# A new layout of the attention phase in front of two MoE layers, with three more weight pieces converted in it and their low parts passed through DRAM

## The chip, the core and the metric

The kernel runs on one core of one Trainium2 chip. The metric is the device time of one execution in microseconds (us), the median of several runs. Lower is better.

## What is computed

Attention over four batches, eight heads, 576 tokens and 64 columns a head, in two parts that are added: attention over queries, keys and values averaged in groups of four tokens (144 of them), repeated four times, and attention within three tokens to either side. Two dense layers follow on the 2304 x 512 result.

```python
out_d = sm_attn(q_d, k_d, v_d)                 # q_d, k_d, v_d: means over 4 tokens
out_up = np.repeat(out_d, factor, axis=2)
mask = np.abs(pos[:, None] - pos[None, :]) < factor
scores = np.where(mask, scale * np.matmul(q, k.transpose(0, 1, 3, 2)), -1000000000.0)
out_local = np.matmul(softmax(scores), v)
x = (out_up + out_local).transpose(0, 2, 1, 3).reshape(2304, 512)
h = x @ w_in;  r = np.maximum(h, 0.0);  x = (r * r) @ w_out          # layer 1, d_ff = 2048
h = x @ w_in2; y = (h * np.cos(h)) @ w_out2                          # layer 2
```

The weights are float64. The kernel turns each into a sum of two 32-bit numbers, a high and a low part.

## The kernel before

Layer 1 is cut into five blocks of tokens (8, 7, 7, 7 and 7 windows of 64 tokens) and 16 weight pieces of 128 hidden columns. A **slot** is one piece in one block: stage A (`stage_a`, 12 matmuls) makes the hidden tile `ps_h`, ScalarE makes `gt` and `gh` of it (`gelem1`, lines 543 and 544, `high`, line 532), VectorE makes `gl` (`low`, line 538), and stage B (`stage_b1`, 12 matmuls) adds to four accumulators. The time from the program's start to the first matmul of slot 0 is called the **first phase** here, and the 16 slots of the first block are **block 0**.

A weight piece is **converted** by `conv1` and `split`: its 1 MB raw tile is loaded by SP (line 413), ScalarE takes the absolute value of the top words into a tile `bits` (line 427), VectorE makes four passes over it (lines 429, 430, 434, 437), ScalarE rounds it to the high part `w1hi` (line 441), and GpSimd subtracts to get the low part in two halves, `loa` and `lob` (line 448), which stay in SBUF for block 0 and are also stored to DRAM (`lo_d`, line 473) for the later blocks. There are two raw tiles and two `bits` tiles.

Attention consists of tasks, written as Python generators that are advanced in turn: `pool` (the sums over four tokens), `down` (attention over these sums, one for each pair of heads; its results are the tiles `xd`, written at line 290) and `window` (the local attention of 64 tokens, four head pairs at once; its last steps add `xd` at line 388 and write the block's inputs `xh` and `xl` at lines 400 and 401). Windows 0 to 7 make block 0. While they are worked on (`early`), large temporary tiles are put into the places of weight pieces that are not yet converted (`spare`, `SPREAD`). `warm` puts matmuls without a use into the first phase: 48 at the start and 8 in each round of the tasks. In the first phase of the kernel before, piece 0 is converted early, piece 1 once six windows are ready and piece 2 once eight are.

Every engine runs its instructions in the order of the program, and that order was made by a list scheduler; DMAs are all issued by SP, in order, and an issue that waits holds back all behind it.

Of the kernel before, what the change touches and what calls it, by code (L numbers as in the profile page):

```python
# [42 lines left out]
AHEAD = 3  # L43
WARM0 = 48
WARM = 8
NA2 = 6
# [21 lines left out]
def kernel(  # L68
# [54 lines left out]
    def need(name, n=1):  # L123
        while early[0] and name in SPREAD:
            if spare:
                held.setdefault(name, []).append(spare.pop(0))
                return
            yield
        while used[name] + n > caps[name]:
            yield  # L130
        used[name] += n

    def done(name, n=1):
        if early[0] and name in SPREAD:
            spare.append(taken[name].pop(0))
        else:
            used[name] -= n

    spare = list(range(AHEAD, NF))
    held, taken = {}, {}  # L140

    def task_tile(name, rows, cols):
        if not early[0]:
            return cm.tile([rows, cols], F32, tag=name, name=name, bufs=caps[name])
        f = held[name].pop(0)
        taken.setdefault(name, []).append(f)
        return wp.tile([P, 2 * DM], F32R, tag=f"hi{f}", name=name).bitcast(F32)[:rows, :cols]
# [32 lines left out]
    def pool(b):  # L180
        yield from need("qp")
        yield from need("vp")
        kp = cm.tile([P, HPAIR, SD], F32, tag="kp", name="kp", bufs=caps["qp"])
        vp = cm.tile([KTOK, 2, DM], F32, tag="vp", name="vp", bufs=caps["vp"])
        parts = [(i, hp) for hp in range(HPAIR) for i in range(2)]
        parts += [((0, 1), hp) for hp in range(HPAIR)] if early[0] else [((kt,), hp) for hp in range(HPAIR) for kt in range(2)]
        loaded = []
        for i, hp in parts:
            yield from need("pl")
            if isinstance(i, int):  # L190
                t = task_tile("pl", P, S)
# [8 lines left out]
            if not early[0] and len(loaded) == 2:  # L200
                yield
                while loaded:
                    pool_sum(*loaded.pop(0), kp, vp)
                    done("pl")
        for piece in loaded:
            pool_sum(*piece, kp, vp)
            done("pl")
        pooled[b] = (qp, kp, vp)

    def pool_sum(*piece):  # L210
# [3 lines left out]
    def pool_piece(i, hp, t, kp, vp):  # L214
# [9 lines left out]
        else:  # L224
# [3 lines left out]
            )  # L228

    def down(b, hp):  # L230
        while b not in pooled:
# [15 lines left out]
        nc.vector.tensor_reduce(out=mx[:, 0], in_=sv, op=ALU.max, axis=AX.X)  # L247
        nc.vector.tensor_tensor(
            out=pr, in0=sv, in1=mx[:, 0].unsqueeze(2).broadcast_to([QROWS, 3, SD]), op=ALU.subtract
        )  # L250
        done_a(s)
        nc.scalar.activation(out=pr, in_=pr, func=AF.Exp, scale=SCALE / FACTOR ** 2)
        yield
        nc.vector.tensor_reduce(out=mx[:, 1], in_=pr, op=ALU.add, axis=AX.X)
        nc.vector.tensor_scalar(
# [51 lines left out]
    def window(w):  # L307
# [19 lines left out]
        for hp in range(HPAIR):  # L327
# [6 lines left out]
        prv = pr[:, :, :n]  # L334
        nc.vector.tensor_reduce(out=mx[:, 0], in_=sv, op=ALU.max, axis=AX.X)
        nc.vector.tensor_tensor(
            out=prv, in0=sv, in1=mx[:, 0].unsqueeze(2).broadcast_to([P, HPAIR, n]), op=ALU.subtract
        )
        done_a(s)
        nc.scalar.activation(out=prv, in_=prv, func=AF.Exp, scale=SCALE)  # L340
        yield
        nc.vector.tensor_reduce(out=mx[:, 1], in_=prv, op=ALU.add, axis=AX.X)
        nc.vector.tensor_scalar_add(out=mx[:, 1], in0=mx[:, 1], scalar1=1e-9)
# [21 lines left out]
        m = w - W0[j]  # L365
        while not early[0] and any((b, hp) not in downs for hp in range(HPAIR)):
            yield
# [86 lines left out]
    def conv1(f, after=0):  # L454
# [12 lines left out]

        for said in split(raw, hi1[f], ring):
            if said:
                done("raw")  # L470
            yield
        for k, lo in enumerate(los):
            nc.sync.dma_start(out=lo_d[f][:, k * DM:(k + 1) * DM], in_=lo.bitcast(F32))
# [197 lines left out]

    for f in range(AHEAD, NF):
        start_at(f - AHEAD - 1, conv1, f)
# [52 lines left out]
    for i in range(n1):  # L726
# [16 lines left out]
        jn, fn = divmod(i + AHEAD, NF)  # L743
        if jn > 0:
            for k in range(2):
# [112 lines left out]
```

## Time and profile before

| quantity | value |
|---|---|
| time, median of 3 runs (lowest to highest) | 1032.32 us (1029.2 to 1035.13) |
| time of the profiled execution | 1029.67 us |
| its span, first to last instruction | 1027.9 us |
| mean granted TensorE clock | 0.976 |
| TensorE matmul busy | 979.8 us, 95% of the span |
| VectorE busy | 615.3 us, 60% |
| ScalarE busy | 455.1 us, 44% |
| GpSimd busy | 140.4 us, 14% |
| first matmul of slot 0 | 90.40 us |

The shares are averages over stages that differ: TensorE is busy nearly always, but part of that is the matmuls without a use, and in the first phase it runs at a lower granted clock at times. VectorE's 60% is a mean of a first phase in which it often waits, a block 0 in which it hardly ever does, and long stretches later in which it has little to do.

### The profile page before, as it was taken

Reading aid. Unit: us, or ns where it says so; the run is one execution under the profiler, and the core shown is the slowest. Engines: PE = TensorE matmul, PEld = TensorE weight load, DVE = VectorE, ACT = ScalarE, POOL = GpSimd, SP = SyncE. Lnnn points to the kernel's source line nnn. Section 1 sums busy time; section 2 is a strip of 40 time slices with the busy share of each in tenths; the row PEclk is TensorE's granted clock in tenths of the full one; section 3 lists DMA queues with packets and bytes.
Section 4 is the critical chain, followed back from the end, with each engine's and each line's share of the span. In section 5 each row is a group of like instructions: output and inputs, shape, how many; then the busy total and the mean of one; then the engine's idle time right before and its main releaser. Section 6 shows DMA issues by size and latency. Waiting matters only on the chain.

```text
span 1027.9 us, 13081 instructions
## 1 busy us (share of the span) xinstructions
PE 979.8 (95%) x4868; PEld 825.8 (80%) x4868; DVE 615.3 (60%) x1062; ACT 455.1 (44%) x789; POOL 140.4 (14%) x112
## 2 busy tenths in 40 slices
PE   7879898889999999999999997999999999999998
PEld 4657677778999899999988895888888888888887
DVE  6628989967456844454227515756556555655565
ACT  2325555544555554444445434434334433433343
POOL 0301655511111221112003200000000000000000
PEclk9869999999999999999999999999999999999999
DMA  9903777775568856676556558001000100000010
GB/s 288 288 0 127 234 248 258 254 257 201 179 217 291 266 183 208 216 243 197 183 188 221 192 167 302 1 1 61 21 1 11 52 1 1 20 21 1 1 42 21
DMA packets 58096, 145.50 MB, mean 142 GB/s; under 512 B 6904, under 2 KB 12152, under 8 KB 53808
## 3 DMA queue, kind: packets, MB, share of 16 engines
q1 hardware_dynamic: 58032, 144.67, 42.2%
q8 instruction: 38, 0.62, 0.3%
q14 instruction: 26, 0.21, 0.1%
HBM read 116.33 MB, written 28.31 MB: 141 GB/s over the span
## 4 chain that ended last, share of the span: by engine, by line
PE 65%; DMA 7%; DVE 5%; ACT 2%; issue 1%; POOL 0%; SPq 0%; DVEq 0%; ACTq 0%
PE ps_h L520 30%; PE acc L578 19%; PE acc L572 11%; DMA pl<-in_pool_v_dram 2%; DMA pl<-in_pool_qk_dram 2%; DMA y_d<-y 2%; PE ps_a L372 1%; PE ps_a L328 1%; DVE bits L437 1%; DVE bits L434 1%; PE ps_a L281 1%; DVE gl L538 1%; DMA raw<-in_w_dram 1%; PE ps_a L355 1%; DVE vp L225 1%
## 5 line engine op out<-in xcount | busy, mean ns | idle before, releaser
L538 DVE TENSOR_TENSOR gl<-gt,gh 128x448 fp32r<-128x448 f32 (+1 forms) x80 | 58.4, 730 | 124.0 <-ACT gh L532 123.7
L520 PE MATMUL ps_h<-xh,w1hi 128*128 128x448 f32 (+1 forms) x320 | 124.1, 388 | 7.9 <-ACT gt L543 6.6
L572 PE MATMUL acc<-gl,w1hi 128*128 128x448 f32 (+1 forms) x320 | 121.4, 379 | 1.1 <-DVE gl L538 1.1
L520 PE MATMUL ps_h<-xh,w2hi 128*128 128x512 f32 (+1 forms) x320 | 118.2, 376 | 3.6 <-DVE r L564 3.6
L520 PE MATMUL ps_h<-xl,w1hi 128*128 128x448 f32 (+1 forms) x320 | 119.8, 374 | 0.0
L520 PE MATMUL ps_h<-xl,w2hi 128*128 128x512 f32 (+1 forms) x320 | 118.2, 376 | 0.0
L578 PE MATMUL acc<-w2hi,gh 128*128 128x512 f32 x288 | 113.9, 396 | 3.1 <-ACT y L587 2.5
L578 PE MATMUL acc<-w2lo,gh 128*128 128x512 f32 x288 | 113.4, 394 | 0.0
L560 ACT ACTIVATE r<-r,half_pi 128x512 f32<-128x512 f32 (+1 forms) x80 | 54.6, 683 | 132.0 <-DVE r L556 132.0
L578 PE MATMUL acc<-w2hi,gl 128*128 128x512 f32 x288 | 112.1, 395 | 0.0
L572 PE MATMUL acc<-gh,w1hi 128*128 128x448 f32 (+1 forms) x320 | 103.5, 381 | 2.3 <-ACT gh L532 2.0
L554 DVE TENSOR_SCALAR u<-u 128x512 f32<-128x512 f32 (+1 forms) x80 | 32.0, 399 | 121.0 <-ACT u L549 120.4
L572 PE MATMUL acc<-gh,lo 128*128 128x448 f32 x256 | 93.2, 364 | 0.0
L520 PE MATMUL ps_h<-xh,w2lo 128*128 128x512 f32 (+1 forms) x320 | 80.5, 372 | 0.0
L543 ACT ACTIVATE gt<-ps_h 128x448 f32<-128x448 f32 (+1 forms) x80 | 44.1, 552 | 76.3 <-PE ps_h L520 75.4
L520 PEld LDWEIGHTS ps_h<-xh,w1hi 128*128 128x128 f32 x320 | 61.2, 191 | 16.9 <-ACT gt L543 8.9
L520 PEld LDWEIGHTS ps_h<-xh,w2hi 128*128 128x128 f32 x320 | 60.6, 189 | 16.4 <-DVE r L564 4.1
L549 ACT ACTIVATE u<-ps_h,quarter 128x512 f32<-128x512 f32 (+1 forms) x80 | 51.5, 644 | 44.0 <-PE ps_h L520 41.6
L520 PEld LDWEIGHTS ps_h<-xl,w2hi 128*128 128x128 f32 x320 | 60.6, 190 | 12.3
L532 ACT ACTIVATE gh<-r 128x512 fp32r<-128x512 f32 (+1 forms) x80 | 47.1, 589 | 50.8 <-DVE r L564 46.0
L572 PEld LDWEIGHTS acc<-gh,w1hi 128*128 128x128 f32 x320 | 60.4, 190 | 10.0 <-ACT gh L532 2.6
L572 PEld LDWEIGHTS acc<-gl,w1hi 128*128 128x128 f32 x320 | 60.9, 190 | 8.8 <-DVE gl L538 2.6
(107 smaller groups left out, 1818.9 us busy)
## 6 DMA issues: line engine op xcount, KB each, us to landing
raw<-in_w_dram SPq DMA_DIRECT2D x32, 1024.0 KB
lo<-lo_d SPq DMA_DIRECT2D x128, 256.0 KB
qkw<-in_win_qk_dram SPq DMA_DIRECT2D x36, 396.0 KB
pl<-in_pool_qk_dram SPq DMA_DIRECT2D x32, 288.0 KB
w_d<-shi SPq DMA_DIRECT2D x10, 512.0 KB
w_d<-bits SPq DMA_DIRECT2D x10, 512.0 KB
w2lo<-w_d SPq DMA_DIRECT2D x10, 512.0 KB
w2hi<-w_d SPq DMA_DIRECT2D x10, 512.0 KB
```

Of the source, the lines that this page charges most:

```text
L225: nc.vector.tensor_reduce(out=vp[:, i[0]:i[-1] + 1, hp * P:(hp + 1) * P], in_=t.rearrange("p (k j r) -> p k j r", k=len(i), r=FACTOR), op= ...
L281: last["pe"] = nc.tensor.matmul(av[:, :2 * SD], vp[:, kt, hp * P:(hp + 1) * P], pt[:, kt], start=kt == 0, stop=kt == 1).ins
L328: last["pe"] = nc.tensor.matmul(sv[:, hp], qw[:, hp], kw[:, hp, :n], start=False, stop=hp == HPAIR - 1).ins
L520: nc.tensor.matmul(h[:, :n], a[:, c * P:(c + 1) * P], x[:, c, :n], start=i == 0, stop=i == len(order) - 1)
L532: nc.scalar.activation(out=gh, in_=gt, func=AF.Copy)
L538: last["gl"] = nc.vector.tensor_tensor(out=gl, in0=gt, in1=gh.bitcast(F32), op=ALU.subtract).ins
L543: last["relu"] = nc.scalar.activation(out=gt, in_=h, func=AF.Relu).ins
L549: nc.scalar.activation(out=u, in_=h, func=AF.Identity, bias=quarter, scale=float(1.0 / (2 * math.pi)))
L554: nc.vector.tensor_scalar(out=u, in0=u, scalar1=MAGIC, scalar2=MAGIC, op0=ALU.add, op1=ALU.subtract)
L560: nc.scalar.activation(out=r, in_=r, func=AF.Sin, bias=half_pi, scale=1.0)
L572: nc.tensor.matmul(acc[d][:, :n], a, x, start=f == 0 and i == 0, stop=f == NF - 1 and i == 2)
L578: nc.tensor.matmul(acc[t], x[:, ts], a[:, DM:2 * DM], start=f == 0 and i == 0, stop=f == NF - 1 and i == 2)
```

## The change

Only the first phase is written anew; the program from block 1 on is the same code.

- **Early softmax.** A new function `exps` is used by `down` and `window`. In the first phase VectorE only takes the maximum and scales it by a negative constant (a tiny operation); ScalarE then reads the scores from PSUM and takes the exponential with that value as bias, one instruction for each of three (`down`) or four (`window`) groups, with the sum as a second output. VectorE's subtraction over the whole tile and its sum over the whole tile go. Windows 8 and 9, which the scheduler also starts in the first phase, keep the old form.
- **Warm matmuls.** 48 become 32 at the start, 8 become 4 in each round.
- **Spare tiles.** The first two or three tiles of each kind of temporary (not `pl`) now come from their own pool; ten places of weight pieces are lent where 13 were, since pieces 3, 4 and 5 are to be converted.
- **Conversions.** Piece 0's is no longer put ahead; pieces 1 and 2 may start their passes once three and five windows are ready, and pieces 3, 4 and 5 (`PRE`) once six are, still in the first phase's task list. The low parts of these three are made in one GpSimd instruction in the `bits` tile, stored to DRAM, and read back by `load_lo` in slots 0, 1 and 2 for slots 3, 4 and 5.
- **Waits.** A window now waits for all `down` tasks of its batch ahead of its last product in the first phase too.
- `pe_pool` is there but never called, as `PE_POOLED` is 0.

```diff
-WARM0 = 48
-WARM = 8
+PRE = 3
+WARM0 = 32
+WARM = 4
+PE_POOLED = 0
...
         while early[0] and name in SPREAD:
+            if name != "pl" and used[name] < caps[name]:
+                used[name] += 1
+                held.setdefault(name, []).append(None)
+                return
...
-    spare = list(range(AHEAD, NF))
+    spare = list(range(AHEAD + PRE, NF))
...
+    def exps(bank, sv, mx, pr, scale):
+        nc.vector.tensor_reduce(out=mx[:, 0], in_=sv, op=ALU.max, axis=AX.X)
+        if early[0]:
+            nc.vector.tensor_scalar_mul(out=mx[:, 0], in0=mx[:, 0], scalar1=-scale)
+            for i in range(sv.shape[1]):
+                nc.scalar.activation(
+                    out=pr[:, i], in_=sv[:, i], func=AF.Exp, bias=mx[:, 0, i:i + 1], scale=scale,
+                    accum_out=mx[:, 1, i:i + 1],
+                )
+            done_a(bank)
+            yield
+            return
+        nc.vector.tensor_tensor(
+            out=pr, in0=sv, in1=mx[:, 0].unsqueeze(2).broadcast_to(list(sv.shape)), op=ALU.subtract
+        )
+        done_a(bank)
+        nc.scalar.activation(out=pr, in_=pr, func=AF.Exp, scale=scale)
+        yield
+        nc.vector.tensor_reduce(out=mx[:, 1], in_=pr, op=ALU.add, axis=AX.X)
...
-        while not early[0] and any((b, hp) not in downs for hp in range(HPAIR)):
+        while any((b, hp) not in downs for hp in range(HPAIR)):
...
-        for said in split(raw, hi1[f], ring):
+        steps, lo = split(raw, hi1[f], None if AHEAD <= f < AHEAD + PRE else ring), None
...
+        if not los:
+            nc.sync.dma_start(out=lo_d[f], in_=lo)
...
-    tasks += [pool(0), conv1(0)]
+    tasks += [pool(0)]
     tasks += [down(0, hp) for hp in range(HPAIR)]
     tasks += [window(w) for w in range(W0[1])]
-    tasks += [conv1(1, W0[1] - 2), conv1(2, W0[1])]
+    tasks += [conv1(0), conv1(1, 3), conv1(2, 5)]
+    tasks += [conv1(f, 6) for f in range(AHEAD, AHEAD + PRE)]
...
-    for f in range(AHEAD, NF):
+    for f in range(AHEAD + PRE, NF):
         start_at(f - AHEAD - 1, conv1, f)
...
-        if jn > 0:
+        if jn > 0 or fn < AHEAD + PRE:
             for k in range(2):
                 load_lo(jn, fn, k)
```

The scheduler's order follows the tasks, so instructions move on every engine. Three places matter. In the names, `dmx` and `mx` are the maxima and sums of `down` and `window`, `dpr` and `pr` their probabilities, `bits` and `raw` the tiles of a conversion, `vw` and `qkw` a window's operands, `pl` the operands of the next batch's `pool`. Lines in rows of the kernel after are its own.

**VectorE, at the scores of the first batch's four `down` tasks.** Before:

```order
L225 TENSOR_REDUCE vp_179<-pl_202 72x2x128
L429 TENSOR_SCALAR bits_359<-bits_359 128x1024
L247 TENSOR_REDUCE dmx_235<-ps_acc_231 96x3
L430 TENSOR_SCALAR bits_359<-bits_359 128x1024
L247 TENSOR_REDUCE dmx_244<-ps_acc_240 96x3
L248 TENSOR_TENSOR dpr_236<-ps_acc_231,dmx_235 96x432
L247 TENSOR_REDUCE dmx_253<-ps_acc_249 96x3
L434 SCALAR_TENSOR_TENSOR bits_359<-raw_228,bits_359 128x1024
L247 TENSOR_REDUCE dmx_262<-ps_acc_258 96x3
L248 TENSOR_TENSOR dpr_245<-ps_acc_240,dmx_244 96x432
```

After:

```order
L268 TENSOR_REDUCE vp_163<-pl_208 72x2x128
L274 TENSOR_REDUCE dmx_217<-ps_acc_213 96x3
L274 TENSOR_REDUCE dmx_228<-ps_acc_224 96x3
L274 TENSOR_REDUCE dmx_239<-ps_acc_235 96x3
L276 TENSOR_SCALAR dmx_217<-dmx_217 96x3
L274 TENSOR_REDUCE dmx_250<-ps_acc_246 96x3
L276 TENSOR_SCALAR dmx_228<-dmx_228 96x3
L276 TENSOR_SCALAR dmx_239<-dmx_239 96x3
L276 TENSOR_SCALAR dmx_250<-dmx_250 96x3
L311 TENSOR_SCALAR dmx_217<-dmx_217 96x3
```

The four passes of piece 0's conversion (`bits_359`) stood between the maxima and no longer do, and the subtractions (`dpr`) are gone.

**ScalarE, at the end of the first phase.** Before, where `gt_762` is slot 0's hidden tile and `bits_816` piece 3:

```order
L358 COPY pt_918<-ps_a_913 67x512
L400 ACTIVATE xh_436<-xt_700 128x4x128
L358 COPY pt_1024<-ps_a_1019 67x512
L441 ACTIVATE w1hi1_682<-bits_683 128x1024
L221 COPY qp_126<-qc_767 64x144 x2
L340 ACTIVATE pr_979<-pr_979 128x280
L543 ACTIVATE gt_762<-ps_h1_735 128x512
L427 ACTIVATE bits_816<-raw_758 128x1024
```

After, where `gt_770` is slot 0's hidden tile, `bits_710` and `bits_723` are pieces 3 and 4 and the last `xh_498` is what slot 0 starts from:

```order
L490 ACTIVATE w1hi1_613<-bits_614 128x1024
L407 COPY pt_682<-ps_acc_677 70x512
L490 ACTIVATE w1hi2_649<-bits_650 128x1024
L476 ACTIVATE bits_710<-raw_654 128x1024
L449 ACTIVATE xh_498<-xt_674 128x4x128
L407 COPY pt_916<-ps_a_911 67x512
L476 ACTIVATE bits_723<-raw_687 128x1024
L264 COPY qp_126<-qc_775 64x144 x2
L490 ACTIVATE w1hi3_709<-bits_710 128x1024
L600 ACTIVATE gt_770<-ps_h1_747 128x512
```

Pieces 1 and 2 are rounded ahead of the block's last `xh`, pieces 3 and 4 stand around it, and the absolute value of piece 3 now stands ahead of that `xh`.

**SP, around the raw loads of pieces 3 and 4.** Before (`raw_758` is piece 3, `vw_985` belongs to a window of block 1):

```order
L312 DMA qkw_474<-in_win_qk_dram 128x792
L317 DMA vw_476<-in_win_v_dram 70x512
L317 DMA vw_985<-in_win_v_dram 70x512
L312 DMA qkw_1157<-in_win_qk_dram 128x792
L413 DMA raw_758<-in_w1_dram 128x2048
L312 DMA qkw_1231<-in_win_qk_dram 128x792
L192 DMA pl_772<-in_pool_qk_dram 128x576
```

After (`raw_654` and `raw_687` are pieces 3 and 4, `raw_727` is piece 5, `vw_970` the window's tile that waits for a first product of block 1's windows):

```order
L368 DMA qkw_1047<-in_win_qk_dram 128x792
L462 DMA raw_654<-in_w1_dram 128x2048
L462 DMA raw_687<-in_w1_dram 128x2048
L530 DMA lo_d1_96<-loa_702 128x512
L530 DMA lo_d1_96<-lob_703 128x512
L530 DMA lo_d2_97<-loa_714 128x512
L530 DMA lo_d2_97<-lob_715 128x512
L201 DMA pl_780<-in_pool_qk_dram 128x576
L373 DMA vw_970<-in_win_v_dram 70x512
L201 DMA pl_782<-in_pool_qk_dram 128x576
L368 DMA qkw_1133<-in_win_qk_dram 128x792
L462 DMA raw_727<-in_w1_dram 128x2048
```

and a little behind it, where the low parts of pieces 3 and 4 are stored and read back:

```order
L462 DMA raw_888<-in_w1_dram 128x2048
L528 DMA lo_d3_98<-bits_710 128x1024
L201 DMA pl_823<-in_pool_qk_dram 128x576
L201 DMA pl_825<-in_pool_qk_dram 128x576
L528 DMA lo_d4_99<-bits_723 128x1024
L538 DMA lo_784<-lo_d3_98 128x512
L538 DMA lo_786<-lo_d3_98 128x512
```

Pieces 3 and 4 are now asked for ahead of the long wait for a window's tile; the reading of `lo_d3` stands behind its own store and waits on SP for it.

## Rows read from the trace of the kernel before

**Rows 1.** Busy time by stretch, us: busy (instructions) per engine, clock, DMA share, GB/s.

```profile
core 0: us, PE busy (x) PEld busy (x) DVE busy (x) ACT busy (x) POOL busy (x), PEclk, DMA share, GB/s
18.10:50.00 31.90, 25.51 (x147) 18.28 (x145) 21.07 (x54) 10.91 (x19) 9.24 (x11) 0.84 0.98 311
50.00:90.40 40.40, 34.22 (x170) 23.92 (x170) 17.88 (x44) 11.89 (x30) 3.22 (x5) 0.75 0.02 5
90.40:230.00 139.60, 124.67 (x606) 99.99 (x606) 122.87 (x176) 77.25 (x131) 64.21 (x41) 0.96 0.75 251
```

**Rows 2.** Timeline, ScalarE: start, duration (us), engine, line, operation, [idle before, releaser].

```profile
73.15 0.57 ACT L290 COPY xd<-ps_acc 64x144 f32<-64x144 f32 x2 [2.38 <-PE ps_acc L281]
...
102.93 1.06 ACT L441 ACTIVATE w1hi<-bits 128x1024 fp32r<-128x1024 f32 x1 [0.84 <-DVE bits L437]
...
208.97 1.06 ACT L441 ACTIVATE w1hi<-bits 128x1024 fp32r<-128x1024 f32 x1 [0.55 <-DVE bits L437]
233.42 0.52 ACT L543 ACTIVATE gt<-ps_h 128x448 f32<-128x448 f32 x1
```

**Rows 3.** Timeline of SP's queue: a long duration is an issue that waits.

```profile
44.86 43.94 SPq L317 DMA_DIRECT2D vw<-in_win_v_dram  x2
...
91.00 0.35 SPq L413 DMA_DIRECT2D raw<-in_w_dram  x1
```

**Rows 4.** Waits of SP's queue, 0 to 200 us: us in total, times, longest.

```profile
SPq L317 <- PE ps_a L372: 43.2, 1, 43.2
```

**Rows 5.** Timeline, VectorE, at the end of the pooling.

```profile
16.83 1.22 DVE L225 TENSOR_REDUCE vp<-pl 72x256 f32<-72x1024 f32 x1 [0.47 <-DMA pl<-in_pool_v_dram]
...
21.18 0.60 DVE L247 TENSOR_REDUCE dmx<-ps_acc 96x3 f32<-96x432 f32 x1
```

**Rows 6.** Groups by form, VectorE, first 90.4 us: count | busy us, mean ns | idle before.

```profile
L388 DVE TENSOR_TENSOR xt<-ps_acc,xd 64x256 f32<-64x256 f32 x16 | 6.6, 421 | 11.3 <-ACT xd L290 9.7 <-PE ps_acc L372 1.3
...
L336 DVE TENSOR_TENSOR pr<-ps_acc,mx 128x280 f32<-128x280 f32 x7 | 3.1, 442 | 0.3
...
L437 DVE SCALAR_TENSOR_TENSOR bits<-raw,bits 128x1024 uint32<-128x1024 uint32 x2 | 2.4, 1218 | 0.0
L434 DVE SCALAR_TENSOR_TENSOR bits<-raw,bits 128x1024 uint32<-128x1024 uint32 x2 | 2.4, 1218 | 0.0
...
L254 DVE TENSOR_REDUCE dmx<-dpr 96x3 f32<-96x432 f32 x4 | 2.3, 581 | 0.0
...
L343 DVE TENSOR_SCALAR mx<-mx 128x4 f32<-128x4 f32 x10 | 2.2, 218 | 0.2
L401 DVE TENSOR_TENSOR xl<-xt,xh 128x512 fp32r<-128x512 f32 x3 | 2.1, 692 | 1.0 <-ACT xh L400 1.0
...
L429 DVE TENSOR_SCALAR bits<-bits 128x1024 f32<-128x1024 f32 x2 | 1.4, 689 | 2.5 <-ACT bits L427 2.5
L430 DVE TENSOR_SCALAR bits<-bits 128x1024 uint32<-128x1024 uint32 x2 | 1.4, 681 | 0.0
```

**Rows 7.** Groups by form, ScalarE, from 90 us to the end.

```profile
L560 ACT ACTIVATE r<-r,half_pi 128x512 f32<-128x512 f32 x64 | 46.5, 726 | 111.8 <-DVE r L556 111.8
...
L532 ACT ACTIVATE gh<-r 128x512 fp32r<-128x512 f32 x64 | 40.4, 632 | 48.0 <-DVE r L564 43.5 <-PE acc L578 4.6
...
L340 ACT ACTIVATE pr<-pr 128x280 f32<-128x280 f32 x21 | 9.1, 435 | 14.4 <-DVE pr L336 14.3
```

**Rows 8.** Chain of waits that ended last: start us, us, what.

```profile
191.99 6.64 DMA raw<-in_w_dram
...
349.81 3.64 DMA y_d<-y
...
710.12 2.81 PE acc L578 x12
```

**Rows 9.** Timeline, TensorE: matmuls without a use, and slot 0's first.

```profile
29.81 5.55 PE L648 MATMUL ps_warm<-const_b 128*128 128x512 bf16 x16
...
90.40 0.50 PE L520 MATMUL ps_h<-xh,w1hi 128*128 128x512 f32 x1
```

More of the change, by code (lines that the diff above doesn't have):

```diff
@@ L133, in done @@
     def done(name, n=1):
-        if early[0] and name in SPREAD:
-            spare.append(taken[name].pop(0))
-        else:
-            used[name] -= n
-    spare = list(range(AHEAD, NF))
+        f = taken[name].pop(0) if early[0] and name in SPREAD else None
+        if f is None:
+            used[name] -= n
+        else:
+            spare.append(f)
+    spare = list(range(AHEAD + PRE, NF))
     held, taken = {}, {}
     def task_tile(name, rows, cols):
-        if not early[0]:
+        f = None
+        if early[0]:
+            f = held[name].pop(0)
+            taken.setdefault(name, []).append(f)
+        if f is None:
             return cm.tile([rows, cols], F32, tag=name, name=name, bufs=caps[name])
-        f = held[name].pop(0)
-        taken.setdefault(name, []).append(f)
         return wp.tile([P, 2 * DM], F32R, tag=f"hi{f}", name=name).bitcast(F32)[:rows, :cols]
@@ L199, in pool, with pe_pool @@
             loaded.append((i, hp, t))
-            if not early[0] and len(loaded) == 2:
+            if len(loaded) < 2:
+                continue
+            if not early[0]:
                 yield
[L202 to L207, printed above, removed]
-        pooled[b] = (qp, kp, vp)
+            if b < PE_POOLED:
+                if not early[0]:
+                    yield
+                bank, = yield from need_a()
+                pe_pool(bank, loaded, kp, vp)
+                done_a(bank)
+                done("pl")
+                done("pl")
+                loaded = []
+            while loaded:
+                pool_sum(*loaded.pop(0), kp, vp)
+                done("pl")
+        pooled[b] = (qp, kp, vp)
+    def pe_pool(bank, pieces, kp, vp):
+        c0 = 0
+        for i, hp, t in pieces:
+            if isinstance(i, int):
+                rows, cols = P, SD
+                tv = t.rearrange("p (j r) -> p r j", r=FACTOR)
+            else:
+                rows, cols = KTOK, len(i) * P
+                tv = t.rearrange("p (c r) -> p r c", r=FACTOR)
+            o = bank[:rows, c0:c0 + cols]
+            c0 += cols
+            for r in range(FACTOR):
+                last["pe"] = nc.tensor.matmul(
+                    o, ident[:rows, :rows], tv[:, r], start=r == 0, stop=r == FACTOR - 1
+                ).ins
+            if i == 0:
+                for a in range(2):
+                    half = slice(a * D, (a + 1) * D)
+                    nc.scalar.copy(out=qp[half, hp, a], in_=o[half])
+            elif i == 1:
+                nc.vector.tensor_copy(out=kp[:, hp], in_=o)
+            else:
+                nc.vector.tensor_copy(
+                    out=vp[:, i[0]:i[-1] + 1, hp * P:(hp + 1) * P], in_=o.rearrange("p (k c) -> p k c", k=len(i))
+                )
     def pool_sum(*piece):
@@ L246, in down @@
         pr = task_tile("dpr", QROWS, 3 * SD).rearrange("p (m s) -> p m s", m=3)
[L247 to L254, printed above, removed]
+        yield from exps(s, sv, mx, pr, SCALE / FACTOR ** 2)
         nc.vector.tensor_scalar(
@@ L334, in window @@
         prv = pr[:, :, :n]
[L335 to L342, printed above, removed]
+        yield from exps(s, sv, mx, prv, SCALE)
         nc.vector.tensor_scalar_add(out=mx[:, 1], in0=mx[:, 1], scalar1=1e-9)
@@ L466, in ring @@
             return los
-        for said in split(raw, hi1[f], ring):
+        steps, lo = split(raw, hi1[f], None if AHEAD <= f < AHEAD + PRE else ring), None
+        while True:
+            try:
+                said = next(steps)
+            except StopIteration as end:
+                lo = end.value
+                break
             if said:
```

4 lines of the change are left out of this document (added).

## Prediction

> **What bounds the kernel now.** I read the busy time by stretch first [rows 1]. Until 90.40 us [rows 9] no layer is computed: between 18 and 90 us VectorE is busy 39 of 72 us, ScalarE 23, GpSimd 12, and the DMA engines stand still after 50 us. No engine bounds this first phase; a chain through PSUM, VectorE, ScalarE and GpSimd does. From 90.40 to 230.00, which is about block 0, VectorE is busy 122.87 of 139.60 us and TensorE 124.67 at a granted clock of 0.96. From then on TensorE has nearly no gap, and the change doesn't touch that part. So the gain must come from the first 233 us, up to block 1's first hidden tile [rows 2].
>
> The second view is ScalarE's timeline [rows 2]. The last `xd` of the first batch is copied at 73.15, piece 2 is rounded at 102.93, when slot 0 has begun, piece 15 at 208.97: (208.97 - 102.93) / 13 = 8.16 us a piece. Sixteen slots of 24 matmuls at 2.81 / 12 = 0.234 us each [rows 8] are 89.9 us, so block 0 is not bound by its own matmuls alone. The third view is SP's queue: one issue, a window's tile, holds it for 43.94 us [rows 3, 4], and piece 3's load stands behind and goes out at 91.00 [rows 3].
>
> **The change part by part: the first phase.** Sums are made against the profiled execution, 1029.67 us (span 1027.9), which is 2.65 below the median of 1032.32.
>
> *Early softmax.* VectorE loses two passes for each of eight windows at 0.442 and for each of four `down` tasks at 0.581 (I take the other pass of each pair at the same price) [rows 6]: 16 x 0.44 + 8 x 0.58 = 11.7 us. It gains twelve scalings of some elements, some 2 us. ScalarE reads 280 columns in four instructions where it took one of 0.435 us. No row has 70 columns. A column costs (0.632 - 0.435) / 232 = 0.85 ns [rows 7], so one without a bias is 0.435 - 210 x 0.00085 = 0.26 us; a bias tile adds 0.726 - 0.632 = 0.09 [rows 7]; four are 1.4 us at most, less what they overlap. Lower bound: the 0.435 of now. I take 1.1, with 0.9 for a `down` task: eight times 0.7 and four times 0.4 more, 7 us on an engine that is busy 23 of 72 [rows 1]. About half of it stands in the chain. The Trainium skill (ScalarE: Activation LUTs, What ACT_TABLE_LOAD costs) gives 280 ns and 0.833 ns a column with a pointer bias, 186 ns without, and this speaks against the split: four times 0.34, 1.35 us. Its difference of 94 ns is what the two rows show; by it the first phase would be 1 to 2 us longer than I say.
>
> *Order.* Before, the first maximum of `down` begins at 21.18, behind the wait for piece 0's absolute values; the pooling ends at 16.83 + 1.22 = 18.05 [rows 5]. Now nothing stands between: 3 us. Four passes over piece 0 (0.689 + 0.681 + 2 x 1.218 = 3.81 us [rows 6]) leave the middle of the four tasks. Walking the new order with the rows' durations, the four exponentials end near 24 us, the scores of three windows near 28, the transposes begin near 30, and the last `xd` comes near 52 rather than at 73.15, as the four tasks no longer stand behind all windows' scores and are not gathered in one row of ping-pong between TensorE and ScalarE. This is the least sure step: 47 to 58.
>
> *Warm matmuls.* Sixteen cost 5.55 us, 0.35 each [rows 9], more than at full speed. Sixteen fewer at the start are hidden by the pooling; four fewer in each round give 1.4 us a round where a round stands in the chain. That is in the walk. What the clock does with fewer is open: it was granted at 0.84 and 0.75 [rows 1], between its two levels of 1.2 and 2.4 GHz, already.
>
> *Behind the last `xd`* VectorE has: sixteen additions at 0.421 (6.7), four `xl` at 0.692 (2.8), pieces 1 and 2 (2 x 3.81 = 7.6), five maxima and four passes of windows 8 and 9 at 0.44 (4.0), some 12 tiny ones at 0.218 (2.6): 23.7 us [rows 6], with 2 to 3 us of waits. Before, it had 17 us there, up to 90.40, with one piece. So 52 + 26 = 78 us for the last `xl`. One new wait: on ScalarE piece 3's absolute value stands ahead of the block's last `xh`, and its raw tile is only asked for when piece 1 has been read, near 73. A load of 1 MB took 6.64 us [rows 8]: 73 + 0.4 + 6.6 + 1.1 + 0.6 = 81.7. I take slot 0 at 81: 9.5 us earlier. Bounds: 76 (the walk's good end), 94 (the `xd` stay where they were, less the early softmax).
>
> **Block 0.** Pieces 3 and 4 follow each other directly, as their loads no longer wait for the window's tile; piece 2 is rounded near 76 instead of 102.93, and I get the later pieces 20 us ahead of now. Their cadence stays, by two `bits` tiles and two raw tiles, so piece 15 comes near 188. Then TensorE and VectorE bound the stretch. TensorE's content is 124.67 - 0.04 x 139.6 = 119 us at full clock [rows 1]; VectorE's is 122.87 less piece 2, 3.8, also 119. Of 139.6 us, 20.6 could go. I take half, 10: VectorE stays over 90% busy, so what comes late from it (the `gl`, the maxima) stays late. Bounds: 0 and 20.
>
> What it adds: three stores of 512 KB that were there already, in two halves, and six readings of 256 KB, 1.6 MB where the DMA share is 0.75 [rows 1]. SP waits for each store before the reading. The nearest row is a store of a block's result, 3.64 us [rows 8]. For slot 3 the low part must be back when TensorE has done 3 slots and the attention between, 20 us or more behind slot 0, at 101 or later. Piece 3 is rounded near 89, subtracted by 92, stored by 97 and read back by 102: just covered. If not, the reading itself, 3.64, is late once or twice.
>
> **Sum.** 9.5 + 10 = 19.5, less 0.5 for a late reading: 19. The profiled execution would be 1010.7, the median 1032.3 - 19 = 1013.
>
> **Rivals.**
> - *Only the first phase is shorter.* Block 0 keeps its length because the cadence of 8.16 us [rows 2] is set by the two `bits` tiles and SP's waits and what is ahead is lost again. For it: pieces 3 to 5 hold a `bits` tile until their store has landed. Against: twelve more pieces would have to lose 20 us together. Time: 1032.3 - 9.5 = 1023.
> - *Block 0 falls to its content.* Both ends good: 9.5 + 20.6 = 30: 1002. Against: VectorE would have to be busy all the time.
> - *The first phase doesn't do what the change says.* The order puts pieces 3 to 5 at the edge of block 0, not into the first phase. If the `xd` come at 73 as now, 26 us follow and slot 0 starts at 99, 8.5 later, while block 0 gains 10: 1031, no change.
> - *Slower: the way through DRAM.* SP issues everything, and it waits for the store of each of three pieces with the raw loads of pieces 7 to 9 behind. A store and a reading are 2 x 3.64 = 7.3 us [rows 8]; if all three stand on the path, 22, and the two `bits` tiles that wait for the stores hold the conversion back too, so that the pieces are no earlier than now and block 0 gains nothing: 22 - 9.5 = 12.5 slower, 1045. It decides from the point at which TensorE reaches slot 3's last four matmuls of stage A before the reading lands, and again in slots 4 and 5. For it: the margin above is about nothing. Against: two pieces follow each other and their stores overlap.
>
> **How the numbers follow.** The forecast 0.55; only the first phase 0.17; block 0 at its content 0.10; no change 0.11; slower 0.07. A measurement tells some 0.5%, 5 us, from no change here. Faster by over 0.5%: 0.55 + 0.17 + 0.10 = 0.82; within 0.11; slower 0.07. The range leaves out the last two, 0.18: from 1002, both gains at their good ends, to 1027, which is 5 us of the first phase and nothing in block 0.
>
> **What would show it.** In the profile after: the last `xd` near 52 us; slot 0's first matmul at 76 to 86; the load of piece 3 issued near 73, and ScalarE's wait for it ahead of the last `xh`; pieces 3 and 4 rounded by 95; piece 15 near 188; block 1's first hidden tile near 214 instead of 233.42; the parts after that as long as now. Wrong it would be if `xd` came after 65, if TensorE waited at slot 3 for a tile `lo`, or if a later block gave the lead back: its attention tasks start by slot numbers and would then be pressed into less time.

## The result and the profile after

The changed kernel took 1023.35 us (median of 6 runs, 1017.78 to 1029.45) where the kernel before, run beside it, took 1031.56 (1029.20 to 1040.09): a ratio of 0.9896, 95% interval 0.9859 to 0.9932. That is 8 us faster by the medians, 7 to 15 by the interval, where 19 were forecast; the time lies within the range. The profiled execution took 1023.16 us with a span of 1021.4 and a mean granted clock of 0.978, 6.5 us less than the profiled execution before.

First the stretches of [rows 1], in the same columns (busy us and instructions of PE, PEld, DVE, ACT and POOL, granted clock, DMA share, GB/s):

```profile
18.10:50.00 31.90, 23.26 (x128) 18.92 (x129) 15.26 (x42) 20.39 (x84) 9.24 (x11) 0.73 0.94 300
50.00:90.40 40.40, 32.65 (x192) 27.13 (x192) 34.57 (x65) 19.37 (x51) 11.09 (x10) 0.79 0.47 152
90.40:230.00 139.60, 125.88 (x619) 101.31 (x618) 118.75 (x178) 73.70 (x129) 49.16 (x35) 0.98 0.76 249
```

Between 50 and 90 us VectorE is now busy 34.57 us, twice as long as before (17.88), and the DMA engines work. Now ScalarE's timeline, for [rows 2]:

```profile
51.07 0.57 ACT L346 COPY xd<-ps_acc 64x144 f32<-64x144 f32 x2 [1.31 <-PE ps_acc L337]
...
75.99 1.13 ACT L476 ACTIVATE bits<-raw 128x1024 f32<-128x1024 f32 x1 [2.66 <-POOL pr L394]
77.02 0.62 ACT L449 ACTIVATE xh<-xt 128x512 fp32r<-128x512 f32 x1
...
86.49 1.06 ACT L490 ACTIVATE w1hi<-bits 128x1024 fp32r<-128x1024 f32 x1 [4.59 <-DVE bits L486]
87.45 0.58 ACT L600 ACTIVATE gt<-ps_h 128x512 f32<-128x512 f32 x1
...
188.19 1.06 ACT L490 ACTIVATE w1hi<-bits 128x1024 fp32r<-128x1024 f32 x1
...
211.60 0.54 ACT L600 ACTIVATE gt<-ps_h 128x448 f32<-128x448 f32 x1 [1.44 <-PE ps_h L577]
```

The last `xd` comes 22 us earlier (73.15 before), piece 15 is rounded 21 us earlier (208.97), block 1's first hidden tile is 22 us earlier (233.42). So up to here the change has done what it says. TensorE's timeline, for [rows 9], shows slot 0:

```profile
77.69 0.79 PE L577 MATMUL ps_h<-xh,w1hi 128*128 128x512 f32 x1 [1.15 <-ACT xh L449]
78.28 1.96 PE L421 MATMUL ps_a<-pt,vw 67*128 67x128 f32 x8
...
82.16 0.78 PE L577 MATMUL ps_h<-xl,w1hi 128*128 128x512 f32 x1
82.74 0.63 PE L577 MATMUL ps_h<-xh,w1hi 128*128 128x512 f32 x1
83.16 0.63 PE L577 MATMUL ps_h<-xl,w1hi 128*128 128x512 f32 x1
```

Slot 0's first matmul is 12.7 us earlier (90.40 before). But attention matmuls stand between it and the second, and then the matmuls follow each other every 0.42 us, at the lower level of the clock (0.54 of full speed is granted between 80 and 85 us). Slot 0's hidden tile was at 94.95 before and is at 87.45: a lead of 7.5 us.

The reading that decides is the same table with its cuts at hidden tiles: slot 0's, block 1's first, slot 64's (the first of block 4). Before, then after, each with both stretches and their sum:

```profile
94.95:233.42 138.47, 122.89 (x596) 98.66 (x595) 121.66 (x175) 75.52 (x128) 61.36 (x40) 0.96 0.75 249
233.42:529.75 296.33, 293.72 (x1658) 271.77 (x1658) 154.79 (x300) 144.04 (x272) 44.83 (x37) 1.00 0.64 214
94.95:529.75 434.80, 416.61 (x2253) 370.43 (x2252) 276.45 (x474) 219.56 (x399) 106.19 (x77) 0.98 0.68 225
```

```profile
87.45:211.60 124.15, 114.14 (x550) 91.23 (x549) 109.68 (x153) 69.95 (x123) 49.22 (x33) 0.97 0.79 261
211.60:522.73 311.13, 303.51 (x1715) 277.91 (x1713) 160.21 (x310) 145.72 (x274) 46.68 (x38) 1.00 0.63 208
87.45:522.73 435.28, 417.64 (x2263) 369.13 (x2261) 269.88 (x463) 215.66 (x397) 95.91 (x71) 0.99 0.67 223
```

Block 0 became 14.3 us shorter, blocks 1 to 3 became 14.8 us longer, and the sum is what it was: 434.80 and 435.28 us. TensorE's busy time says why. Of the 14.3 us, 122.89 - 114.14 = 8.75 are TensorE work that is no longer done in block 0 (550 matmuls in the records instead of 596), and only (138.47 - 122.89) - (124.15 - 114.14) = 5.57 are idle time removed. The attention for later blocks starts by slot numbers; when slots pass faster, less of it fits in. By block 1's first hidden tile 136 of the windows' last products had run before, 17 windows of eight, and 120 after, 15 windows; both had 72 at slot 0's hidden tile. In blocks 1 to 3 TensorE then has 9.8 us more to do and idles 7.6 us instead of 2.6. The lead is 7.5 us at slot 0's hidden tile, 7.0 at slot 64 and 7.1 at slot 79 (614.87 and 607.81).

These 5.0 us of new idle time do not lie in one place. The start of block 1 and the end of block 3, in the same columns:

```profile
211.60:240.00 28.40, 24.65 (x147) 21.85 (x146) 17.43 (x38) 12.51 (x23) 3.17 (x4) 1.00 0.57 180
...
505.00:522.73 17.73, 15.98 (x86) 14.68 (x84) 4.05 (x9) 6.39 (x12) 0.00 (x0) 1.00 0.57 194
```

TensorE idles 3.75 us in the first (2.5 of them in one wait for an accumulator of block 0 that ScalarE has yet to empty) and 1.75 in the second. For the second, the chain of waits shows the cause (start us, us, what):

```profile
512.75 0.44 DVE xl L450
...
513.26 7.15 DMA x<-y_d
...
520.63 2.19 ACT xh L747 x4
522.83 0.43 ACT gt L600
```

and the list of waits (us in total, times, longest) of the end of layer 1:

```profile
ACT xh L747 <- DMA x<-y_d: 5.0, 1, 5.0
```

The tile for layer 2's first input `x` lies in the memory of the attention's pool, so its load must wait for the last window's `xl` (512.75), and lands 7.15 us later. ScalarE, which takes `x` apart at line 747, has that ahead of slot 64's hidden tile in its order and waits 5.0 us. TensorE still has work for most of that time and then waits 2.3 us for the hidden tile (1.75 of them before 522.73):

```profile
523.30 0.47 PE L577 MATMUL ps_h<-xh,w1hi 128*128 128x448 f32 x1 [2.33 <-ACT gt L600]
```

Before, the load was issued at 510.05, 20 us ahead of slot 64's hidden tile, and nothing waited for it.

### The profile page after: what moved, and what is told of

It reads as the page before. It is cut to its first block, busy times and chain, and to the rows that moved or that the text cites. A ratio compares the mean times of both kernels' runs of the same rounds, so it can differ in the third digit from the quotient of the medians.

```text
span 1021.4 us, 13061 instructions
## 1 busy us (share of the span) xinstructions
PE 966.7 (95%) x4824; PEld 819.3 (80%) x4824; DVE 613.0 (60%) x1050; ACT 463.1 (45%) x865; POOL 134.2 (13%) x109
## 4 chain that ended last, share of the span: by engine, by line
PE 68%; DVE 13%; DMA 12%; ACT 3%; issue 3%; POOL 1%; SPq 0%; DVEq 0%; ACTq 0%; POOLq 0%
PE ps_h L577 29%; PE acc L635 19%; PE acc L629 11%; DMA pl<-in_pool_v_dram 4%; DMA pl<-in_pool_qk_dram 3%; DVE bits L483 3%; DMA y_d<-y 2%; DVE bits L486 2%; PE ps_a L421 1%; PE ps_a L384 1%; DMA raw<-in_w_dram 1%; DVE xt L437 1%; DVE gl L595 1%; DVE bits L479 1%; DVE bits L478 1%
## 5 line engine op out<-in xcount | busy, mean ns | idle before, releaser
L629 PE MATMUL acc<-gh,w1hi 128*128 128x448 f32 (+1 forms) x320 | 98.7, 380 | 3.9 <-ACT y L644 3.3
L629 PE MATMUL acc<-gh,lo 128*128 128x448 f32 (+1 forms) x268 | 98.6, 368 | 0.0
```

What stands on the lines that cost most here:

```text
L629: nc.tensor.matmul(acc[d][:, :n], a, x, start=f == 0 and i == 0, stop=f == NF - 1 and i == 2)
```

## The experiments

**Theory A**: the gain is the earlier slot 0; block 0's lead is real but is given back, as work that comes later and as the wait for `x` at block 4, because the windows are tied to slot numbers. **Theory B**: the gain comes from block 0 and its three more pieces, and what the first phase gains counts little. The later rivals stand in the expectations. All ratios are against the kernel before on the same chip.

| run | us, median | ratio (95% interval) |
|---|---|---|
| changed kernel | 1023.35 | 0.9896 (0.9859 to 0.9932) |
| no_extra_pieces | 1022.20 | 0.9913 (0.9878 to 0.9947) |
| old_softmax | 1025.94 | 0.9941 (0.9920 to 0.9961) |
| old_warm | 1025.01 | 0.9930 (0.9905 to 0.9955) |
| windows_earlier | 1016.00 | 0.9849 (0.9821 to 0.9877) |
| before_windows_earlier | 1034.74 | 1.0039 (1.0009 to 1.0068) |
| windows_earlier_still | 1016.43 | 0.9861 (0.9823 to 0.9899) |
| input_converted_later | 1024.47 | 0.9933 (0.9907 to 0.9959) |
| no_extra_pieces_windows_earlier | 1021.08 | 0.9898 (0.9871 to 0.9925) |
| old_softmax_windows_earlier | 1021.76 | 0.9877 (0.9855 to 0.9898) |
| old_warm_windows_earlier | 1021.52 | 0.9873 (0.9853 to 0.9894) |
| fewer_warm_windows_earlier | 1033.98 | 1.0014 (0.9988 to 1.0040) |
| layout_only_windows_earlier | 1015.25 | 0.9813 (0.9781 to 0.9845) |

And from the profiled execution of each: start of the hidden tile `gt` (us) of slot 0, block 1 and slot 64, the time from the first to the last of these, TensorE's busy time in it, and the time at which piece 3 is rounded.

| run | slot 0 | block 1 | slot 64 | 0 to 64 | busy | piece 3 |
|---|---|---|---|---|---|---|
| before | 94.95 | 233.42 | 529.75 | 434.80 | 416.61 | 112.65 |
| before_windows_earlier | 97.42 | 232.38 | 533.76 | 436.34 | 418.82 | 115.89 |
| changed kernel | 87.45 | 211.60 | 522.73 | 435.28 | 417.64 | 86.49 |
| windows_earlier | 88.10 | 215.83 | 516.02 | 427.92 | 415.16 | 87.14 |
| windows_earlier_still | 85.72 | 216.13 | 517.95 | 432.23 | 417.11 | 84.75 |
| no_extra_pieces_windows_earlier | 83.21 | 217.47 | 520.05 | 436.84 | 418.04 | 105.00 |
| old_softmax_windows_earlier | 85.12 | 220.47 | 520.96 | 435.84 | 418.12 | 94.59 |
| old_warm_windows_earlier | 86.27 | 222.13 | 521.62 | 435.35 | 417.44 | 93.29 |
| layout_only_windows_earlier | 80.31 | 214.71 | 516.03 | 435.72 | 418.08 | 97.06 |
| fewer_warm_windows_earlier | 94.09 | 224.65 | 531.21 | 437.12 | 419.95 | 95.72 |

### One part of the change undone

```diff
-PRE = 3
+PRE = 0
```

> The kernel after with PRE = 0: no piece goes through DRAM, pieces 3 to 5 are converted in block 0 as before the change, and thirteen spare places are lent again; the rest of the new layout stays. Theory A (the gain of the change is the shorter first phase, 90.40 to 77.69 us, and the three pieces that are converted ahead give block 0 little, as its cadence is set by VectorE and the two tiles): 1020 to 1027, with slot 0 within 3 us of 77.7. Theory B (the lead of three pieces is what makes block 0 earlier): slot 0 as early, but block 1's first hidden tile 8 us or more later than 211.6, and 1030 or more.

Measured: 1022.20 us, the same as with the pieces. As A expected, what they give block 0 is not there at the end. This kernel's profiled execution was its slowest (1030.03), with slot 0's first matmul at 85.50, its hidden tile at 91.98 and block 1's first at 227.70, so the marks that the theories name can't be judged by it; more on that below.

```diff
-        if early[0]:
+        if False:
```

> The kernel after with the softmax of the kernel before in the first phase too (maximum, subtraction and sum on VectorE, one exponential for all groups); the layout, the pieces and the warm matmuls are those of after. Theory A (VectorE's 11.7 us of passes stand in the chain of the first phase): slot 0 5 to 9 us later, at 83 to 87, and 1027 to 1032. Theory B (the order of the tasks alone makes the first phase shorter; what VectorE loses, ScalarE gets): slot 0 within 3 us of 77.7 and 1021 to 1026.

Measured: 1025.94, 2.6 us more than the changed kernel, at the upper end of B's range, and the two intervals overlap. Slot 0's first matmul came 4 us later (81.64), between the two theories, but its hidden tile 2.6 us earlier (84.89).

```diff
-WARM0 = 32
-WARM = 4
+WARM0 = 48
+WARM = 8
```

> The kernel after with 48 and 8 warm matmuls as before the change. Theory A (four more in each of about ten rounds stand in TensorE's chain at 0.24 to 0.43 us each, but part of the rounds wait for something else): slot 0 3 to 8 us later, 1026 to 1031. Theory B (with fewer warm matmuls the clock is granted lower in the first phase, 0.73 where it was 0.84, and that costs as much): slot 0 within 2 us of 77.7, the clock from 18 to 50 us back above 0.8, 1021 to 1025.

Measured: 1025.01, 1.7 more, at the upper end of B's range, with intervals that overlap. Slot 0's first matmul was at 80.49 and its hidden tile at 83.57, 3.9 us earlier than in the changed kernel, and that lead was gone at slot 64 (522.28), where ScalarE waits 2.6 us for `x` as well. Neither part alone carries the gain.

### The windows started earlier

```diff
-        start_at(m if j == 1 else NF * (j - 1) - 6 + 2 * m, window, w)
+        start_at(m if j == 1 else NF * (j - 1) - 8 + 2 * m, window, w)
```

> The kernel after with the windows of blocks 2 to 4 started two slots earlier (NF * (j - 1) - 8 + 2 * m in place of - 6). Theory A (the change puts two windows behind; the last window then ends next to block 4, layer 2's first input can only be loaded behind it, and ScalarE stands 5.0 us before its conversion with the hidden tile of slot 64 behind): that wait falls to under 1 us, the lead over the kernel before at the end of layer 1 is 11 us or more instead of 7, 1016 to 1020. Theory B (TensorE's work is the same and what is saved there is lost elsewhere): 1021 to 1025.

Measured: 1016.00. In its trace, SP's queue and ScalarE's timeline at block 4 read:

```profile
489.23 0.32 SPq L739 DMA_DIRECT2D x<-y_d  x1
```

```profile
511.66 2.18 ACT L747 ACTIVATE xh<-x 128x512 fp32r<-128x512 f32 x4
516.02 0.55 ACT L600 ACTIVATE gt<-ps_h 128x448 f32<-128x448 f32 x1 [1.09 <-PE ps_h L577]
```

The load goes out at 489.23, 27 us ahead of slot 64's hidden tile, and nobody waits for it. The time from slot 0 to slot 64 fell by 7.4 us: 4.9 of TensorE's idle time and 2.5 of its busy time. The idle time went in both places, at the start of block 1 and ahead of slot 64's hidden tile:

```profile
215.83:240.00 24.17, 24.17 (x153) 22.26 (x152) 17.78 (x40) 13.00 (x26) 4.63 (x5) 1.00 0.63 194
...
505.00:516.02 11.02, 11.02 (x57) 10.34 (x56) 3.75 (x6) 5.38 (x11) 0.00 (x0) 1.00 0.34 120
```

So the edit takes the wait for `x` away, as A says, but on TensorE that wait is 1.75 us of these, and 3.75 come from the start of block 1, which A did not name (the other stretches idle 0.6 more). How much of the 7.35 us by the medians the wait for `x` is worth is not shown.

> The kernel before, with the windows of blocks 2 to 4 started two slots earlier (the same edit as in windows_earlier) and nothing else. Theory A: the edit only takes away a wait that the changed kernel has at the start of block 4, and the kernel before has no wait for layer 2's input there: 1029 to 1034, no difference. Theory C: earlier windows are worth something by themselves, whatever the first phase: 1023 to 1027, as much as the 7 us that the edit gave the changed kernel.

The same edit on the kernel before brought nothing: 1.0039, if anything slower. Earlier windows are not better by themselves. Nor is a shorter first phase enough: without the three pieces the same edit brought nothing clear of noise (0.9913 and 0.9898), while it gained with the old softmax (0.9941 and 0.9877), where no trace shows a wait for `x`.

> The changed kernel with the windows of blocks 2 to 4 four slots earlier than it has them (NF * (j - 1) - 10 + 2 * m). Theory A: at two slots earlier the wait for layer 2's input is already gone, so there is nothing more to take: 1014 to 1018, lead at slot 64 as in windows_earlier (about 14 us). Theory C (earlier is better by itself): 1008 to 1012.

Two slots earlier still (`- 10`): 1016.43, no more to take, as A expected. The lead at slot 64 in its profiled execution is 11.8 us, not 14.

```diff
-        if i == n1 - 8:
+        if i == n1 - 3:
             first_x2 = x2_stream(0)
```

> The changed kernel, with layer 2's first input begun five slots later in the program's list (n1 - 3 for n1 - 8), which puts its rounding on ScalarE behind slot 64's hidden tile; windows as they are. Theory A: what costs is that ScalarE, which has hidden tiles to make, waits 5 us for that input; with the rounding behind them the wait is gone or falls where nothing waits: 1017 to 1020. Rival: the load lands no earlier, and the wait only moves to the next slot or the first of layer 2: 1022 to 1025.

Measured: 1024.47, no gain; the rival was right that the wait only moves, here to slot 66. Slot 64's hidden tile is no longer held up (519.65), but two of the loads of `x` now stand on SP's queue ahead of the stores of block 3's results. The chain:

```profile
527.91 0.62 SPq L739
...
529.29 5.17 DMA y_d<-y
...
534.56 0.64 DVE y L646
...
535.24 2.49 PE acc L629 x11
```

Stage B waits for accumulators whose results cannot leave, and slot 66's hidden tile is at 537.76 (534.15 in the changed kernel).

### What the parts are worth with the give-back removed

Each of these has the windows two slots earlier, and one or two parts of the change undone by the edits above.

> The changed kernel without its three more pieces (PRE = 0), with the windows of blocks 2 to 4 two slots earlier. No_extra_pieces was as fast as the changed kernel, and its trace had no wait for layer 2's input. Theory A: the three pieces do shorten block 0 by 4 to 8 us, and that was given back at block 4, so that with the wait gone they show: 1020 to 1024 here against the 1016.0 of windows_earlier. Rival: the pieces gain nothing at the end in any case: 1014 to 1018, the same as windows_earlier.

> Windows_earlier with the old softmax in the first phase (VectorE subtracts and sums again). Its slot 0 should begin near 81.5, as in old_softmax (81.64 against 77.69). Theory A (the shorter first phase is worth its microseconds once nothing is given back at block 4): 1018 to 1021 against the 1016.0 of windows_earlier. Rival: slots after the first phase take the loss up: 1015 to 1017.

> Windows_earlier without the three more pieces and with the old softmax: left of the change are the pools for temporary tiles, the fewer warm matmuls and the earlier conversions of pieces 1 and 2. No_extra_pieces_windows_earlier was 1021.1. If the parts add up (three pieces 5 us, softmax 2 to 5 us): 1023 to 1026. If what the softmax gains is only useful for the three pieces, whose passes take VectorE's freed time: 1020 to 1022, no more than without the pieces alone.

Measured, as ratios: with both parts 0.9849; without the pieces 0.9898; without the new softmax 0.9877; without either 0.9813. The first two single steps went the way A expected (5 us more without the pieces; 3 to 6 without the softmax, where the intervals overlap). The third refutes the sum: without both, the kernel is 1015.25 us, where the sum expected 1023 to 1026 and the other reading 1020 to 1022. Added to the rest, the new softmax alone and the pieces alone make the kernel slower, by 9 and 7 us by the ratios, and both together leave it where it is, within the intervals. The second table suggests how, with one execution for each kernel: the three pieces put slot 0's hidden tile 4.8 and 4.9 us later, with either softmax, since their passes on VectorE come ahead of it. They repay this between slot 0 and slot 64 only with the new softmax (427.92 against 435.72 to 436.84): then pieces 3 and 4 are rounded around slot 0's hidden tile, with the old one 9 to 11 us behind it. It is the order more than the softmax that goes with the shorter time: old_warm_windows_earlier and fewer_warm_windows_earlier have the new softmax and the pieces too, round piece 3 behind slot 0's hidden tile (93.29 after 86.27, 95.72 after 94.09) and take 435.35 and 437.12 us. Another execution with the rounding ahead, windows_earlier_still, takes 432.23, half of the difference. No run moved the rounding alone. ScalarE of windows_earlier, then of old_softmax_windows_earlier:

```profile
87.14 1.06 ACT L490 ACTIVATE w1hi<-bits 128x1024 fp32r<-128x1024 f32 x1 [4.78 <-DVE bits L486]
88.10 0.58 ACT L600 ACTIVATE gt<-ps_h 128x512 f32<-128x512 f32 x1
91.97 1.06 ACT L490 ACTIVATE w1hi<-bits 128x1024 fp32r<-128x1024 f32 x1 [1.30 <-DVE bits L486]
```

```profile
85.12 0.60 ACT L600 ACTIVATE gt<-ps_h 128x512 f32<-128x512 f32 x1 [0.39 <-PE ps_h L577]
...
94.59 1.04 ACT L490 ACTIVATE w1hi<-bits 128x1024 fp32r<-128x1024 f32 x1
96.45 1.06 ACT L490 ACTIVATE w1hi<-bits 128x1024 fp32r<-128x1024 f32 x1 [0.29 <-DVE bits L486]
```

So the gain is there without the two named parts. What is left is the rest of the new layout (own tiles for temporaries, piece 0's conversion no longer ahead, pieces 1 and 2 earlier, the windows' wait for all `down` tasks, fewer warm matmuls) with the windows of blocks 2 to 4 two slots earlier; without these earlier starts it was not run. With it alone the last `xd` is at 49.34 and slot 0's hidden tile 17 us earlier than in before_windows_earlier. Which of these gives how much was not tried, except for the warm matmuls:

> Windows_earlier with 48 and 8 warm matmuls again for 32 and 4. Slot 0 should begin near 80.5, as in old_warm. Theory A: 1018 to 1020, the 2.8 us at slot 0 kept to the end. Rival (the warm matmuls give back with a higher granted clock, 0.92 against 0.79, what they take): 1015 to 1017.

> Windows_earlier with 16 warm matmuls at the start and 2 in each round, half of what the changed kernel has. If the queueing of the warm matmuls is what is left to take in the first phase: slot 0 at 75 to 77, 1013 to 1015. If the granted clock, which falls with fewer of them (0.73 in 18.10:50.00 now), costs more than they do: slot 0 at 78 to 85, 1016 to 1022.

The old number of warm matmuls: 1021.52, a little more than A's 1018 to 1020; 16 and 2 of them: 1033.98, far worse than either theory thought. By the ratios the old number costs 2.5 us, and the intervals overlap. In its trace slot 0's first matmul was at 83.19, not near 80.5, and the hidden tile 1.8 us earlier than in windows_earlier, so what it loses it loses between slot 0 and slot 64, not at slot 0 as A says. The stretches 18.10 to 50.00 and 50.00 to 90.40 of old_warm_windows_earlier, then of fewer_warm_windows_earlier:

```profile
18.10:50.00 31.90, 24.27 (x148) 17.29 (x147) 15.55 (x41) 19.66 (x82) 10.20 (x11) 0.89 0.89 289
50.00:90.40 40.40, 33.92 (x220) 27.07 (x219) 30.88 (x64) 19.57 (x52) 9.28 (x9) 0.92 0.44 145
```

```profile
18.10:50.00 31.90, 26.18 (x115) 20.86 (x116) 10.83 (x37) 18.90 (x78) 9.14 (x11) 0.61 0.88 284
50.00:90.40 40.40, 33.75 (x150) 29.14 (x150) 26.38 (x58) 15.95 (x45) 8.74 (x9) 0.54 0.35 118
```

With fewer of them the granted clock stays close to its lower level (0.54 is a little over half of 2.4 GHz), TensorE gets through 150 matmuls in the second stretch, where it was 194 in windows_earlier, and all that waits for it comes later. Slot 0's hidden tile is 6 us later than in windows_earlier, slot 64's 15 us; 9 of these are lost behind slot 0, where the order differs too.

The best kernels are windows_earlier and layout_only_windows_earlier, 16 to 19 us faster than before; their intervals overlap.

## Why the prediction was right and wrong

**Right.** Faster, and inside the range, though 10 us short of the 1013 that was forecast. The last `xd` (51.07; forecast 52), slot 0's first matmul (77.69; 76 to 86), the load of piece 3 (issued at 70.56; near 73), pieces 3 and 4 rounded (86.49 and 91.32; by 95), piece 15 (188.19; 188) and block 1's first hidden tile (211.60; 214) all came as forecast. The late reading was priced at 0.5 us, and TensorE waited 0.3 us for `lo`, so the rival through DRAM falls. One thing that it named is in the trace: ScalarE waits 2.3 us for the store of a low part (`lo_d<-bits`) before it takes up the next piece at 98.78. The wait for piece 3's load ahead of the last `xh` came too. The row at 75.99 puts its 2.66 us down to GpSimd, but GpSimd's last reading of that `bits` tile had ended at 74.59, and by the trace's semaphore records the load landed at 75.88, 5.3 us after its issue. The last `xt` was ready at 75.52 and its `xh` began at 77.02, so this order cost slot 0 some 1.5 us.

**Right in part by luck.** The walk let the first maximum of `down` come 3 us earlier, at 18, as nothing of piece 0 stood ahead of it. It came at 20.75 instead of 21.18, because the pooling itself, behind its loads, ended at 20.83 instead of 18.05:

```profile
19.61 1.22 DVE L268 TENSOR_REDUCE vp<-pl 72x256 f32<-72x1024 f32 x1 [0.21 <-DMA pl<-in_pool_v_dram]
20.75 1.62 DVE L274 TENSOR_REDUCE dmx<-ps_acc 96x3 f32<-96x432 f32 x3
```

So the walk was 3 us ahead of the kernel there, and `xd` came at the forecast time all the same. Piece 15 came as forecast, but not by the terms named: piece 2 near 76 and thirteen more at 8.16 us make 182, and what made it 188.19 was piece 2 at 72.27 with a cadence that did not stay, 8.92 us.

**The price of an exponential.** I took 1.1 us for a window's four and 0.9 for a `down` task's three. ScalarE's timeline shows two of the four exponentials of a window:

```profile
28.41 0.32 ACT L278 ACTIVATE pr<-ps_acc,mx 128x70 f32<-128x70 f32 x1 [0.26 <-DVE dmx L311]
28.63 0.19 ACT L278 ACTIVATION_READ_ACCUMULATOR pr<-ps_acc,mx 128x1 f32 x1
28.72 0.31 ACT L278 ACTIVATE pr<-ps_acc,mx 128x70 f32<-128x70 f32 x1
```

They begin 0.29 to 0.31 us apart, 1.2 for four; the 12 of the `down` tasks 0.36 apart, 1.1 for three, a little more than I took. The Trainium skill (ScalarE: Activation LUTs, What ACT_TABLE_LOAD costs) states 280 ns and 0.833 ns a column for an activation with a pointer bias, and that back-to-back ones overlap by about 93 ns. An estimate from both is 0.34 us for one of 70 columns, 0.25 from one to the next and 1.1 for four; the 1.35 in the prediction left the overlap out. The measurement lies a little above the estimate with the overlap, with a sum output behind each exponential.

**Wrong: what the early softmax is for.** The step counted 11.7 us off VectorE and let the walk's 21 us at `xd` depend on it in part. With the old softmax the last `xd` is at 49.88 instead of 51.72 (old_softmax_windows_earlier and windows_earlier), so the 21 us come from the rest of the layout. Slot 0's first matmul is 3.7 us earlier with the new softmax (77.81 and 81.52), but its hidden tile 3.0 us later (88.10 and 85.12).

**Wrong: the mark at which the first phase ends.** The step "I take slot 0 at 81: 9.5 us earlier" was measured at the first matmul. That gained 12.7, the hidden tile 7.5: attention matmuls went in between, and the clock was at its lower level. "What the clock does with fewer is open" was a term without a price. The two windows of the trace, of the changed kernel and then of layout_only_windows_earlier, show it:

```profile
65.00:70.00 5.00, 0.53 (x3) 0.47 (x4) 4.94 (x9) 1.06 (x3) 0.65 (x1) 0.76 0.00 0
70.00:75.00 5.00, 4.18 (x15) 2.47 (x13) 4.89 (x10) 2.58 (x3) 3.19 (x3) 0.50 0.67 231
75.00:80.00 5.00, 3.43 (x13) 2.82 (x14) 2.84 (x5) 2.12 (x3) 3.42 (x4) 0.50 0.94 296
```

```profile
75.00:80.00 5.00, 5.00 (x34) 4.39 (x33) 4.10 (x9) 1.75 (x4) 0.85 (x1) 1.00 0.87 289
```

In the changed kernel VectorE works without a break on windows and passes, TensorE has 0.53 us of work in five, the clock falls to its lower level and slot 0 runs there; in the other it is at full clock by then.

**Wrong: block 0's 10 us as a gain at the end.** "TensorE's content is 124.67 - 0.04 x 139.6 = 119 us at full clock" and "Of 139.6 us, 20.6 could go" took the work in a stretch of time as if it belonged to block 0. Part of it is attention for later blocks, which is only put off. What block 0 could truly give is its idle time of 15.6 us; it gave 5.6, and 5.0 were lost again in blocks 1 to 3: at the start of block 1, in between, and in the wait for `x`. The sentence "the parts after that as long as now" failed (14.8 us longer), and the condition named under it, that a later block gives the lead back because its attention starts by slot numbers, is what happened: more attention is left for blocks 1 to 3. It should have been a rival with a price: 9.5 us at slot 0 and nothing in block 0 is 1023. That is the number of the rival "only the first phase is shorter", but by another mechanism: the cadence of the pieces did slow, from 8.16 to (188.19 - 72.27) / 13 = 8.92 us, and yet block 0 was 14 us shorter.

**Open.** Why the new softmax without the pieces is slower than the old one (0.9898 against 0.9813) isn't settled: its traces differ by 2.9 us at slot 0's hidden tile and 4.0 at slot 64's, in one execution each. Nor is why earlier windows also gained with the old softmax, whose trace shows no wait for `x`: there the time from slot 0 to slot 64 is 438.89 and 435.84 us, and 2.7 of these 3 us are TensorE's busy time, about as much busy time as they took from the changed kernel.

## What to carry to other kernels

Before a gain in one stage is added to the sum, ask whether the bounding engine's busy time over the whole remaining chain falls, or only moves: cut the trace at the same piece of work, not at the same time, and compare busy and idle on both sides. Work that is started by step numbers comes later in relation when steps pass faster, so after a gain upstream its start numbers must be set anew, and the first thing that needs the freed memory behind it tells whether they were. Undo parts in pairs as well as singly: here two parts looked worth 3 to 6 us each, and nothing together.

## What was not expected of the hardware

The sum output of an activation is an instruction of its own in the trace: `ACTIVATION_READ_ACCUMULATOR`, 0.19 to 0.25 us each, which overlaps the activations on either side; 44 of them in the first phase, 9.4 us by their own durations, 32 of them between 18.10 and 50.00 us, are part of why ScalarE's busy time between 18.10 and 50.00 us rose from 10.91 [rows 1] to 20.39 us.

The same instructions took different times in the first phase, at a different granted clock. no_extra_pieces and no_extra_pieces_windows_earlier have the same order of instructions on TensorE, ScalarE and VectorE there. In their profiled executions, in this order, the stretch from 55 to 60 us was:

```profile
55.00:60.00 5.00, 5.00 (x25) 4.82 (x25) 1.69 (x4) 0.49 (x2) 0.00 (x0) 0.50 0.42 122
```

```profile
55.00:60.00 5.00, 4.56 (x41) 4.17 (x40) 4.92 (x10) 2.25 (x10) 0.00 (x0) 1.00 0.36 113
```

The first was granted the lower level from 45 to 60 us without a break, with TensorE's rows full from 45 us on (5.00 of 5.00), the second came up to full clock between 45 and 50 us. Slot 0's hidden tile was at 91.98 in the one and at 83.21 in the other, 8.8 us apart, about the whole effect that was looked for. So a single profile of such a phase says less than it seems to, and the runs of one kernel spread by 10 us and more, the slower ones mostly at a lower mean clock (of the 12 of fewer_warm_windows_earlier, 1026.98 us at 0.966 and 1039.34 at 0.949).
